# A four-stage kernel of attention, soft experts and a feed-forward network: where the copy of the key rows and the queries' transposing DMA stand, and how the value tails are loaded

## The chip, the cores and the metric

One core of a Trainium2 chip. The metric is the device time of one launch in microseconds (us); three runs of the kernel before took 892.85, 893.1 and 895.21 us, median 893.1.

## The reference

Block-causal attention over 8 batches of 8 heads (576 positions, 64 wide), then a soft mixture of 8 experts with 4 slots each, then a feed-forward network with a squared ReLU:

```python
scores = scale * np.matmul(q, k.transpose(0, 1, 3, 2))
scores = np.where(block_i >= block_j, scores, -1000000000.0)   # blocks of 64 positions
attn = np.exp(scores - np.max(scores, axis=-1, keepdims=True))
attn = attn / (np.sum(attn, axis=-1, keepdims=True) + 1e-09)
x = np.matmul(attn, v)                       # to [4608, 512]
logits = x @ phi                             # 32 slots
d = softmax over the tokens; slot_input = d.T @ x
slot_out[e] = np.maximum(slot_input[e] @ w1[e], 0.0) @ w2[e]
x = softmax over the slots (logits) @ slot_out
h = np.maximum(x @ w_in, 0.0); out = h * h @ w_out
```

## The kernel before, in words

Attention works on pairs of heads: pair n is batch n // 4, and in it heads j and 4 + j with j = n % 4, so there are 32 pairs. A function `pair(n)` (L958) writes one step of a pipeline down: the scores and exponentials of pair n, the row maxima of pair n + 2 (`maxpass`), the preparation of pair n + 3 (`split`), the product with the values of pair n - 1 (`pv`), and the loads of later pairs. It has eight slots; each has some functions to call, then up to four loads from a list `dq` (`loads(LR)`), then bits of other work.

The scores of a pair are two matmuls that add up in PSUM: `s1` against `t1` (the transposed keys, high and low parts, and the transposed high parts of the queries), and `s2` against `t2` (L528). `s1` comes from a transposing DMA of `ka` (L425). `s2` is a copy, by a DMA from SBUF to SBUF, of the first 64 rows of `s1`; its other rows are constants (L925). `t2` comes from a transposing DMA of `qb` (L513), which holds the low parts of the queries, the mask and the row maxima; so it can't start before `maxpass` has ended in `fin`. There are two homes for `s2`, one for each parity of n, and one `t2` for each parity: the DMAs that fill them for pair n wait until the scores of pair n - 2 have been read.

In the kernel before `fin` (slot 5 of pair n - 2) issues the transposing DMA for pair n, and pair n - 1 puts the copy for pair n at the head of the load list in slot 2 (L1040). The values of a pair lie in a home of 640 columns, four such homes taking turns: 4 x 128 rows per head, and the last 64 rows ("tail") of both heads by two DMAs of 64 rows of 64 numbers (L311), one per head, for every pair.

TensorE's instructions stand in the order in which the program writes them (`manual_schedule`, L1059). For the other engines a scheduler chooses the order from what is ready by its own account, with the program's order as the preference; SyncE's queue, from which all these DMAs go out in order, is made by it. Each instruction there waits for its own semaphores, and everything behind it waits too.

The weights of the experts (32 chunks of 1 MB) go through a ring of buffers, many of them memory that attention has given back: `wchunks` (L899) adds their loads when a pool is closed, for instance `st_b` and `st_m` at pair 31. The experts and then the feed-forward network follow when attention is over.

Of the kernel before, what the change touches and what calls it, by code (L numbers as in the profile page):

```python
# [10 lines left out]
F16 = mybir.dt.float16  # L11
# [12 lines left out]
def tile_attn_soft_moe_ffn(  # L24
# [97 lines left out]
        return dict(q=t[:, 0], k=t[:, 1])  # L122

    def v_tile(n):
        c0 = 512 * V0 + 640 * (n % 4)
        return ar_hi[:, c0:c0 + 640].rearrange("p (a h d) -> p a h d", h=2, d=D)

    def wchunk(i):
        kind, g, c = wlist[i]
# [106 lines left out]
    def attention():  # L236
# [63 lines left out]
        def load_v(n):  # L300
            b, j = divmod(n, NJ)
            t = v_tile(n)

            def main(hp):
                nc.sync.dma_start(
                    out=t[:, 0:NU, hp, :], in_=v[b][NJ * hp + j, 0:128 * NU, :].rearrange("(u p) d -> p u d", p=128)
                )

            def tail():
                for h in range(2):  # L310
                    nc.sync.dma_start(out=t[64 * h:64 * h + 64, NU, 0, :], in_=v[b][NJ * h + j, 128 * NU:S, :])  # L311

            return [lambda: main(0), tail, lambda: main(1)]

        def load_phi(hp):
            nc.sync.dma_start(
# [76 lines left out]
        def split(n):  # L393
# [45 lines left out]

            return [high_q, lambda: [turn_q(0, 8), turn_q(8, NBLK)], prep_k, low_q]  # L440

        def maxpass(n):
            t1, s1 = T[n][0], T[n][1]
            pmt = pm[n % 2]
            pf = pmt.rearrange("p a b -> p (a b)")
            ptl = sm_p.tile([128, 5], F32, tag="ptl", name="ptl")
            box = {}

            def part(ps, hp, u, c0):
                nc.tensor.matmul(  # L450
                    ps[:, c0:c0 + 128 * (u + 1)].rearrange("p (s c) -> p s c", c=128), t1[:, 2 * u + hp, :],
                    s1[:, hp:2 * u + 2:2, :], start=(c0 == 0), stop=False,
                )

            def mask(ps, c0, step, cnt):
                o = ps[:, 0:512].rearrange("p (a x) -> p a x", x=128)
                o = o[:, c0 // 128:c0 // 128 + (cnt - 1) * (step // 128) + 1:max(step // 128, 1), 64:128]
                nc.tensor.matmul(o, mrow_l, mrow_r[:, 0:1].to_broadcast([128, 64 * cnt]), start=False, stop=True)  # L458

            def red(ps, o, w, cnt=None):  # L460
                i = ps[:, 0:w].rearrange("p (a x) -> p a x", x=min(128, w))
                if cnt:
                    i = ps[:, 0:w].rearrange("p (c a x) -> p c a x", c=cnt, x=128)
                nc.vector.tensor_reduce(out=o, in_=i, axis=AX.X, op=ALU.max)  # L464

            def chunk(i):
                ps = ps_r.tile([128, 512], F32, tag="r", name="ps_max")
                box[i] = ps
                if i < 2:
                    part(ps, i, 0, 0)  # L470
                    part(ps, i, 2, 128)
                    mask(ps, 0, 384, 2)
                    red(ps, pf[:, 8 * i + 3:8 * i + 7], 512)
                elif i == 2:
                    part(ps, 0, 1, 0)
                    part(ps, 1, 1, 256)
                    mask(ps, 128, 256, 2)
                    red(ps, pmt[:, 4:6, 0:2], 512, 2)
                elif i < 5:
                    part(ps, i - 3, 3, 0)  # L480
                    mask(ps, 384, 128, 1)
                    red(ps, pmt[:, 3 + i, :], 512)
                else:
                    for hp in range(2):
                        h0 = 64 * hp
                        nc.tensor.matmul(
                            ps[h0:h0 + 64, 0:512].rearrange("p (s c) -> p s c", c=128) if i == 5
                            else ps[h0:h0 + 64, 0:64],
                            t1[:, 8, h0:h0 + 64],
                            s1[:, hp:8:2, :] if i == 5 else s1[:, 8, h0:h0 + 64],  # L490
                            start=True, stop=True,
                        )
                    red(ps, ptl[:, 0:4] if i == 5 else ptl[:, 4:5], 512 if i == 5 else 64)

            def fin():
                mx = box[4][:, 0:NBLK]
                mv = mx[:, 0:8].rearrange("p (u h) -> p h u", h=2)
                pv4 = pmt.rearrange("p (a b) c -> p a b c", b=2)
                nc.vector.tensor_reduce(out=mv[:, :, 0:3:2], in_=pv4[:, 0:2], axis=AX.X, op=ALU.max)
                nc.vector.tensor_reduce(  # L500
                    out=mv[:, :, 1:4:2].rearrange("p h u -> p u h"), in_=pv4[:, 2:4], axis=AX.X, op=ALU.max
                )
                nc.vector.tensor_reduce(out=mx[:, 8:9], in_=ptl, axis=AX.X, op=ALU.max)
                t = qb[n % NBQ]
                nc.vector.tensor_scalar(
                    out=t[:, :, 64:65], in0=mx.unsqueeze(2), scalar1=-1.0 / SHIFT, scalar2=None, op0=ALU.mult
                )
                nc.vector.scalar_tensor_tensor(
                    out=t[:, :, 65:66], in0=mx.unsqueeze(2), scalar=-1.0 / SHIFT, in1=t[:, :, 64:65],
                    op0=ALU.mult, op1=ALU.subtract,  # L510
                )
                t2 = (mid, odd)[n % 2].tile([128, NBLK, 128], F16, tag="t2", name="t2")
                nc.sync.dma_start_transpose(out=t2, in_=t.rearrange("p s c -> p (s c)"))  # L513
                T[n][2] = t2

            return [lambda i=i: chunk(i) for i in range(5)] + [fin, lambda: [chunk(5), chunk(6)]]

# [66 lines left out]
        def pv(n):  # L584
# [22 lines left out]
            def tl(t):  # L607
                if t == 0:
                    box["tl"] = ps_v.tile([128, 384], F32, tag="tl", name="tl")
                for hp in range(2):  # L610
                    b_, c_ = pp[hp, 1], pp[hp, 2]
                    r = (b_[:, 0:64], b_[:, 448:512], c_[:, 256:320], c_[:, 448:512], pp["d"][:, hp, :])[t]
                    nc.tensor.matmul(  # L613
                        box["tl"][64 * hp:64 * hp + 64, 320:384], vs[:, t, hp if t < NU else 0, :], r,
                        start=(t == 0), stop=False,
                    )

# [340 lines left out]
        def pair(n):  # L958
# [61 lines left out]
            def at_(i, *fs):  # L1020
                slot.setdefault(i, []).extend(f for f in fs if f)
# [9 lines left out]
            if n == 1:  # L1031
                at_(3, sp[2])
                at_(4, sp[0])
                at_(7, sp[1], sp[3])
            else:
                at_(4, get(sp, 3))
            for i in range(8):
                for f in slot.get(i, []):
                    f()
                if i == 2 and n + 1 < N:  # L1040
                    dq.insert(0, lambda: s2copy(n + 1))
                loads(LR)
                f = aux.pop(0) if aux else None
                if f:
# [605 lines left out]
```

## Time and profile before

| | |
|---|---|
| profiled execution | 892.94 us |
| its span, first to last instruction | 891.2 us |
| mean granted TensorE clock | 0.981 |
| TensorE matmuls busy | 824.0 us (92%) |
| VectorE, ScalarE busy | 668.3 us (75%), 627.6 us (70%) |
| GpSimd busy | 253.9 us (28%) |
| queue q1 (all DMAs of SyncE), packet time | 52.1% of 16 engines' span |

Attention ends at about 440 us of the span, the experts take to about 493, the feed-forward network the rest. The rows below use PE for TensorE, DVE for VectorE, ACT for ScalarE, POOL for GpSimd and SPq for SyncE's queue. L12 is line 12 of the kernel. An engine's busy time is not its value: what counts is which wait ends last.

### The profile page before, as it was taken

Reading aid. Unit: us, or ns where it says so; the run is one execution under the profiler, and the core shown is the slowest. Engines: PE = TensorE matmul, PEld = TensorE weight load, DVE = VectorE, ACT = ScalarE, POOL = GpSimd, SP = SyncE. Lnnn points to the kernel's source line nnn. Section 1 sums busy time; section 2 is a strip of 40 time slices with the busy share of each in tenths; the row PEclk is TensorE's granted clock in tenths of the full one; section 3 lists DMA queues with packets and bytes.
Section 4 is the critical chain, followed back from the end, with each engine's and each line's share of the span. In section 5 each row is a group of like instructions: output and inputs, shape, how many; then the busy total and the mean of one; then the engine's idle time right before and its main releaser. Section 6 shows DMA issues by size and latency. Waiting matters only on the chain.

```text
span 891.2 us, 22012 instructions
## 1 busy us (share of the span) xinstructions
PE 824.0 (92%) x8788; PEld 613.5 (69%) x8788; DVE 668.3 (75%) x1600; ACT 627.6 (70%) x1012; POOL 253.9 (28%) x394
## 2 busy tenths in 40 slices
PE   2778998999999999988997799999999999999997
PEld 1446766656676767665633444788888888888887
DVE  5756777968888888952552999788878888888880
ACT  5478776767878777643313789987788888887870
POOL 0234746648584848563200000000000000000000
PEclk9889999999999999998999899999999999999999
DMA  8887899989889789496999600100010000000002
GB/s 167 158 160 154 165 194 163 198 180 191 165 193 185 174 155 187 95 241 159 327 369 382 274 0 1 48 25 25 26 47 25 25 25 25 25 25 25 25 25 48
DMA packets 222023, 113.18 MB, mean 127 GB/s; under 512 B 193760, under 2 KB 195808, under 8 KB 221920
## 3 DMA queue, kind: packets, MB, share of 16 engines
q1 hardware_dynamic: 219264, 111.12, 52.1%
q8 instruction: 69, 1.13, 0.5%
q10 hardware_dynamic: 2656, 0.66, 0.4%
q14 instruction: 34, 0.28, 0.1%
HBM read 78.71 MB, written 9.44 MB: 99 GB/s over the span
## 4 chain that ended last, share of the span: by engine, by line
PE 65%; DMA 9%; DVE 8%; POOL 7%; ACT 6%; issue 2%; SPq 2%; ACTq 0%
PE ps_y L1464 14%; PE ps_x L1464 9%; PE ps_z L1464 9%; PE xm L602 7%; PE po L1486 4%; PE ps_hb L1428 3%; POOL ss L572 3%; DMA s<-ka 3%; PE ps_sc L529 3%; POOL ul L712 3%; DVE pm L464 3%; PE tl L613 2%; DMA wch<-in_moe_w_dram 2%; PE ps_h L1155 2%; PE ps_max L450 2%
## 5 line engine op out<-in xcount | busy, mean ns | idle before, releaser
L1464 PEld LDWEIGHTS <-ah 128*128 128x128 f16 x1792 | 170.3, 98 | 21.9
L567 ACT ACTIVATE p<-ps_sc,es 128x512 f32<-128x512 f32 x192 | 129.0, 695 | 41.7 <-PE ps_sc L529 25.9
L1397 DVE TENSOR_TENSOR al<-a,ah 128x1024 f16<-128x1024 f32 (+1 forms) x128 | 138.7, 1126 | 16.7 <-ACT ah L1451 15.3
L464 DVE TENSOR_REDUCE pm<-ps_max 128x4 f32<-128x512 f32 x160 | 108.6, 684 | 50.2 <-PE ps_max L458 49.4
L572 POOL TENSOR_TENSOR ss<-p 128x384 f32<-128x384 f32 (+1 forms) x128 | 94.4, 758 | 170.3 <-ACT p L567 169.9
L1451 ACT CAST ah<-a 128x1024 f16<-128x1024 f32 (+1 forms) x128 | 114.4, 936 | 15.0 <-DVE a L1397 13.6
L1557 POOL TENSOR_TENSOR ot<-u,p 128x256 f32<-128x256 f32 x16 | 12.4, 778 | 374.6 <-DVE u L1528 338.9
L529 PE MATMUL ps_sc<-t,s 128*128 128x512 f16 (+3 forms) x512 | 106.4, 302 | 13.0 <-DMA s<-s 6.8
L1464 PE MATMUL ps_y<-bh,ah 128*128 128x256 f16 x384 | 104.9, 273 | 0.0
L1464 PE MATMUL ps_y<-bh,al 128*128 128x256 f16 x384 | 104.7, 273 | 0.0
L1464 PE MATMUL ps_y<-bl,ah 128*128 128x256 f16 x384 | 104.7, 273 | 0.0
L572 POOL TENSOR_TENSOR ss<-ss,p 128x320 f32<-128x320 f32 (+1 forms) x128 | 101.1, 790 | 11.8 <-ACT p L567 3.1
L1319 ACT ACTIVATE r<-ps_hb,alpha 128x1024 f32<-128x1024 f32 x64 | 71.2, 1112 | 34.1 <-PE ps_hb L1428 33.4
L1464 PEld LDWEIGHTS <-al 128*128 128x128 f16 x896 | 87.5, 98 | 10.1
L602 PE MATMUL xm<-p,ar_hi 128*64 128x256 f32 (+3 forms) x512 | 93.8, 466 | 0.0
L1397 DVE TENSOR_TENSOR a<-a 128x256 f32<-128x256 f32 x192 | 76.1, 424 | 3.9
L450 PE MATMUL ps_max<-s,t 128*128 128x128 f16 (+3 forms) x256 | 62.3, 309 | 9.7 <-DMA s<-ka 8.2
L1464 PE MATMUL ps_x<-bh,ah 128*128 128x256 f16 x256 | 70.1, 274 | 0.0
L1464 PE MATMUL ps_z<-bh,ah 128*128 128x256 f16 x256 | 70.0, 273 | 0.0
L1464 PE MATMUL ps_z<-bh,al 128*128 128x256 f16 x256 | 69.8, 273 | 0.0
L1464 PE MATMUL ps_x<-bh,al 128*128 128x256 f16 x256 | 69.8, 273 | 0.0
L1464 PE MATMUL ps_x<-bl,ah 128*128 128x256 f16 x256 | 69.8, 273 | 0.0
(255 smaller groups left out, 1827.7 us busy)
## 6 DMA issues: line engine op xcount, KB each, us to landing
wch<-in_moe_w_dram SPq DMA_DIRECT2D x18, 1024.0 KB, 11.0
ar_hi<-in_v_dram SPq DMA_DIRECT2D x64, 128.0 KB, 3.0
raw<-in_moe_w_in_dram SPq DMA_DIRECT2D x16, 512.0 KB, 4.9
out_dram<-ot SPq DMA_DIRECT2D x32, 256.0 KB, 2.2
ar_hi<-in_moe_w_dram SPq DMA_DIRECT2D x6, 1024.0 KB, 8.9
s<-s SPq DMA_DIRECT2D x32, 144.0 KB, 3.5
ar_lo<-in_k_dram SPq DMA_DIRECT2D x32, 128.0 KB, 3.7
ar_hi<-in_k_dram SPq DMA_DIRECT2D x32, 128.0 KB, 3.3
```

The costliest lines, as they stand in the source:

```text
L450: nc.tensor.matmul(ps[:, c0:c0 + 128 * (u + 1)].rearrange("p (s c) -> p s c", c=128), t1[:, 2 * u + hp, :], s1[:, hp:2 * u + 2:2, :], star ...
L464: nc.vector.tensor_reduce(out=o, in_=i, axis=AX.X, op=ALU.max)
L529: nc.tensor.matmul(ps[:, c0:c0 + w].rearrange("p (s c) -> p s c", c=128), kk[:, 2 * t + hp, :], qq[:, 2 * u0 + hp:8:2, :], start=(c0 == 0 ...
L567: exps[:] = [nc.scalar.activation(out=pt, in_=ps, func=AF.Exp, scale=es[:, 0:1])]
L572: add = lambda o, x, y: nc.gpsimd.tensor_tensor(out=o, in0=x, in1=y, op=ALU.add)
L602: nc.tensor.matmul(box["xm"][64 * hp:64 * hp + 64, 128 * t:512], vs[:, t, hp, :], r, start=(t == 0), stop=(t == 3),)
L712: add = lambda o, x, y: nc.gpsimd.tensor_tensor(out=o, in0=x, in1=y, op=ALU.add)
L1319: nc.scalar.activation(out=r[:, c0:c1], in_=ps[:, c0:c1], func=AF.Relu, **kw)
L1397: sub = lambda o, a, b: nc.vector.tensor_tensor(out=o, in0=a, in1=b, op=ALU.subtract)
L1451: nc.scalar.copy(v(hl[n % 2][0][:, 2 * kq:2 * kq + 2], s), v(a7[n, kq], s))
L1464: nc.tensor.matmul(acc[:, 0:HM], a[:, k], b[:, k], start=bool(first and k + j == 0), stop=(k == KH - 1 and j == 2), skip_group_check=not f ...
L1486: nc.tensor.matmul(pos[t], g[:, 512 * a + 128 * t:512 * a + 128 * t + 128], tt[:, c, a], start=(c == 0 and a == 0), stop=(c == KH - 1 and ...
```

## The change

The copy to `s2` for pair n + 1 is written at the head of pair n, before slot 0, and no longer goes through the load list. The queries' transposing DMA becomes a function of its own, `turn_qb`; for pairs 0 and 1 it is still called by `fin`, for all others at the head of pair n for pair n + 1, right behind the copy. The values' homes shrink to 512 columns, and the tails of a whole batch (four pairs) lie in a home of 256 columns, two of them taking turns; they are loaded by two DMAs of 64 rows of 4 x 64 numbers when the first pair of a batch is loaded. The bytes are the same.

```diff
--- before.py
+++ after.py
@@ -122,8 +122,12 @@
         return dict(q=t[:, 0], k=t[:, 1])
 
     def v_tile(n):
-        c0 = 512 * V0 + 640 * (n % 4)
-        return ar_hi[:, c0:c0 + 640].rearrange("p (a h d) -> p a h d", h=2, d=D)
+        c0 = 512 * (V0 + n % NJ)
+        return ar_hi[:, c0:c0 + 512].rearrange("p (a h d) -> p a h d", h=2, d=D)
+
+    def v_tail(b):
+        c0 = 512 * (V0 + NJ) + 256 * (b % 2)
+        return ar_hi[:, c0:c0 + 256].rearrange("p (j d) -> p j d", d=D)
 
     def wchunk(i):
         kind, g, c = wlist[i]
@@ -306,11 +310,13 @@
                     out=t[:, 0:NU, hp, :], in_=v[b][NJ * hp + j, 0:128 * NU, :].rearrange("(u p) d -> p u d", p=128)
                 )
 
-            def tail():
-                for h in range(2):
-                    nc.sync.dma_start(out=t[64 * h:64 * h + 64, NU, 0, :], in_=v[b][NJ * h + j, 128 * NU:S, :])
-
-            return [lambda: main(0), tail, lambda: main(1)]
+            def tail(hp):
+                nc.sync.dma_start(
+                    out=v_tail(b)[64 * hp:64 * hp + 64],
+                    in_=v[b][NJ * hp:NJ * hp + NJ, 128 * NU:S, :].rearrange("j i d -> i j d"),
+                )
+
+            return [lambda: main(0)] + [lambda hp=hp: tail(hp) for hp in range(2) if j == 0] + [lambda: main(1)]
 
         def load_phi(hp):
             nc.sync.dma_start(
@@ -438,6 +444,11 @@
                 nc.scalar.copy(t1[:, s0:s1_, :].rearrange("p s c -> p (s c)"), ps[:, 0:128 * (s1_ - s0)])
 
             return [high_q, lambda: [turn_q(0, 8), turn_q(8, NBLK)], prep_k, low_q]
+
+        def turn_qb(n):
+            t2 = (mid, odd)[n % 2].tile([128, NBLK, 128], F16, tag="t2", name="t2")
+            nc.sync.dma_start_transpose(out=t2, in_=qb[n % NBQ].rearrange("p s c -> p (s c)"))
+            T[n][2] = t2
 
         def maxpass(n):
             t1, s1 = T[n][0], T[n][1]
@@ -509,9 +520,8 @@
                     out=t[:, :, 65:66], in0=mx.unsqueeze(2), scalar=-1.0 / SHIFT, in1=t[:, :, 64:65],
                     op0=ALU.mult, op1=ALU.subtract,
                 )
-                t2 = (mid, odd)[n % 2].tile([128, NBLK, 128], F16, tag="t2", name="t2")
-                nc.sync.dma_start_transpose(out=t2, in_=t.rearrange("p s c -> p (s c)"))
-                T[n][2] = t2
+                if n < 2:
+                    turn_qb(n)
 
             return [lambda i=i: chunk(i) for i in range(5)] + [fin, lambda: [chunk(5), chunk(6)]]
 
@@ -611,7 +621,7 @@
                     b_, c_ = pp[hp, 1], pp[hp, 2]
                     r = (b_[:, 0:64], b_[:, 448:512], c_[:, 256:320], c_[:, 448:512], pp["d"][:, hp, :])[t]
                     nc.tensor.matmul(
-                        box["tl"][64 * hp:64 * hp + 64, 320:384], vs[:, t, hp if t < NU else 0, :], r,
+                        box["tl"][64 * hp:64 * hp + 64, 320:384], vs[:, t, hp, :] if t < NU else v_tail(b)[:, j, :], r,
                         start=(t == 0), stop=False,
                     )
 
@@ -1034,11 +1044,13 @@
                 at_(7, sp[1], sp[3])
             else:
                 at_(4, get(sp, 3))
+            if n + 1 < N:
+                s2copy(n + 1)
+                if n:
+                    turn_qb(n + 1)
             for i in range(8):
                 for f in slot.get(i, []):
                     f()
-                if i == 2 and n + 1 < N:
-                    dq.insert(0, lambda: s2copy(n + 1))
                 loads(LR)
                 f = aux.pop(0) if aux else None
                 if f:
```

The order of TensorE and GpSimd is the same in both kernels, VectorE's differs in two places and ScalarE's in one, all in the first pairs. SyncE's differs throughout. Names: `s2_0`, `s2_1` are the two homes of the copy, `s1` the transposed keys, `t2` the transposed queries, `wch` and `ar_hi<-in_moe_w1` weights of the experts.

The end of attention on SyncE, from the keys' transposing DMA for pair 31 on; before:

```order
L425 DMA_TRANSPOSE s1_7002<-ka_7000 128x9x128
L311 DMA ar_hi_75<-in_v_dram 64x64 x2
L305 DMA ar_hi_75<-in_v_dram 128x4x64
L167 DMA ar_hi_75<-in_moe_w1_dram 128x4x512 x2
L513 DMA_TRANSPOSE t2_7184<-qb0_138 128x9x128
L167 DMA wch_7201<-in_moe_w1_dram 128x4x512
L167 DMA wch_7202<-in_moe_w1_dram 128x4x512
L925 DMA s2_0_141<-s1_6761 64x1152
L167 DMA ar_hi_75<-in_moe_w1_dram 128x2x512
L167 DMA wch_7438<-in_moe_w1_dram 128x4x512
L513 DMA_TRANSPOSE t2_7408<-qb1_139 128x9x128
L925 DMA s2_1_142<-s1_7002 64x1152
```

and now:

```order
L431 DMA_TRANSPOSE s1_6956<-ka_6954 128x9x128
L309 DMA ar_hi_75<-in_v_dram 128x4x64
L171 DMA ar_hi_75<-in_moe_w1_dram 128x4x512 x2
L935 DMA s2_0_141<-s1_6717 64x1152
L450 DMA_TRANSPOSE t2_7156<-qb0_138 128x9x128
L171 DMA wch_7153<-in_moe_w1_dram 128x4x512
L171 DMA wch_7154<-in_moe_w1_dram 128x4x512
L171 DMA ar_hi_75<-in_moe_w1_dram 128x2x512
L935 DMA s2_1_142<-s1_6956 64x1152
L171 DMA wch_7388<-in_moe_w1_dram 128x4x512
L450 DMA_TRANSPOSE t2_7390<-qb1_139 128x9x128
```

The copy for pair 30 (into `s2_0`) stood behind the transposing DMA for pair 30 and two weight chunks, and now stands ahead of all three; the copy for pair 31 (into `s2_1`), which was the last DMA of attention, stands ahead of one chunk and of the transposing DMA for pair 31.

SyncE around the transposing DMA for pair 9 (`qb0`) and the keys' one for pair 11 that follows it; before:

```order
L305 DMA ar_hi_75<-in_v_dram 128x4x64
L311 DMA ar_hi_75<-in_v_dram 64x64 x2
L305 DMA ar_hi_75<-in_v_dram 128x4x64
L925 DMA s2_1_142<-s1_1744 64x1152
L165 DMA ar_hi_75<-in_moe_w1_dram 128x512
L513 DMA_TRANSPOSE t2_2181<-qb0_138 128x9x128
L327 DMA ar_lo_71<-in_k_dram 128x4x64 x2
L334 DMA ar_lo_71<-in_q_dram 64x4x64 x2
L425 DMA_TRANSPOSE s1_2217<-ka_2215 128x9x128
```

and now:

```order
L309 DMA ar_hi_75<-in_v_dram 128x4x64 x2
L169 DMA ar_hi_75<-in_moe_w1_dram 128x512
L333 DMA ar_lo_71<-in_k_dram 128x4x64 x2
L333 DMA ar_lo_71<-in_q_dram 128x4x64 x2
L935 DMA s2_1_142<-s1_1730 64x1152
L169 DMA ar_hi_75<-in_moe_w1_dram 128x512
L450 DMA_TRANSPOSE t2_2203<-qb0_138 128x9x128
L333 DMA ar_lo_71<-in_k_dram 128x4x64
L340 DMA ar_lo_71<-in_q_dram 64x4x64 x2
L333 DMA ar_lo_71<-in_k_dram 128x4x64
L431 DMA_TRANSPOSE s1_2201<-ka_2199 128x9x128
```

The two DMAs for the value tails are gone from here, and loads of keys, queries and weights that came later stand in this stretch; between the two transposing DMAs at its end there are four loads, as before.

## Rows read from the trace of the kernel before

**Rows 1.** Waits of TensorE, whole span: us in total, times, longest.

```profile
PE ps_max L450 <- DMA s<-ka: 8.2, 5, 2.9
...
PE ps_sc L529 <- DMA s<-s: 6.8, 3, 5.3
...
PE ps_sc L529 <- DMA t<-qb: 4.6, 1, 4.6
```

**Rows 2.** Timeline of TensorE, pair 30: start, us, line, work, idle before.

```profile
398.14 0.38 PE L529 MATMUL ps_sc<-t,s 128*128 128x512 f16 x1
...
403.86 0.61 PE L529 MATMUL ps_sc<-t,s 128*128 128x512 f16 x1 [5.35 <-DMA s<-s]
...
410.56 0.28 PE L639 MATMUL tl<-pd,ones 128*32 128x64 f32 x8
...
418.19 0.61 PE L529 MATMUL ps_sc<-t,s 128*128 128x512 f16 x2
```

**Rows 3.** Timeline of SyncE's queue, end of attention.

```profile
383.34 0.99 SPq L167 DMA_DIRECT2D ar_hi<-in_moe_w_dram  x2
386.99 3.85 SPq L513 DMA_TRANSPOSE t<-qb  x1
390.94 2.10 SPq L167 DMA_DIRECT2D wch<-in_moe_w_dram  x2
393.09 1.70 SPq L925 DMA_DIRECT2D s<-s  x1
...
401.55 2.75 SPq L513 DMA_TRANSPOSE t<-qb  x1
...
416.66 1.49 SPq L167 DMA_DIRECT2D wch<-in_moe_w_dram  x3
```

**Rows 4.** Landings: L513 of 386.99, L925 of 393.09, L513 of 401.55.

```profile
DMA to landing us min/median/max: 9.0/9.0/9.0
...
DMA to landing us min/median/max: 10.7/10.7/10.7
...
DMA to landing us min/median/max: 7.2/7.2/7.2
```

**Rows 5.** Windows: us, busy (instructions) of each engine, clock, DMA share, GB/s.

```profile
403.80:411.00 7.20, 7.14 (x72) 4.07 (x73) 0.00 (x0) 1.35 (x3) 0.00 (x0) 0.56 0.78 161
411.00:418.00 7.00, 6.22 (x76) 4.37 (x74) 3.56 (x12) 4.66 (x11) 5.14 (x8) 1.00 0.04 10
...
463.00:468.00 5.00, 5.00 (x48) 1.50 (x48) 0.22 (x1) 0.00 (x0) 0.00 (x0) 1.00 1.05 384
```

**Rows 6.** The chain that ended last, in the experts.

```profile
465.63 14.58 DMA wch<-in_moe_w_dram
```

**Rows 7.** Timeline of TensorE, pair 29, from value product to sums.

```profile
385.60 1.05 PE L602 MATMUL xm<-p,ar_hi 128*64 128x512 f32 x4
...
389.03 0.29 PE L639 MATMUL tl<-pd,ones 128*32 128x64 f32 x8
```

**Rows 8.** Timeline of GpSimd, partial sums of pair 29.

```profile
400.82 1.52 POOL L572 TENSOR_TENSOR ss<-ss,p 128x320 f32<-128x320 f32 x2
```

**Rows 9.** Waits of TensorE in 70 to 90 and in 125 to 150.

```profile
PE ps_sc L529 <- DMA s<-s: 1.5, 2, 1.1
...
PE ps_max L450 <- DMA s<-ka: 2.4, 1, 2.4
```

**Rows 10.** Timeline of SyncE's queue, pairs 0 and 8.

```profile
29.22 0.51 SPq L925 DMA_DIRECT2D s<-s  x1
...
130.51 1.66 SPq L513 DMA_TRANSPOSE t<-qb  x1
...
134.85 2.33 SPq L425 DMA_TRANSPOSE s<-ka  x1
```

**Rows 11.** The tails' DMAs: issue time in ns, min/median/max.

```profile
L311 SPq DMA_DIRECT2D ar_hi<-in_v_dram x64: 472/587/1401, 12.7 to 382.0; - x64
```

**Rows 12.** Timeline of VectorE, low keys of pair 11.

```profile
129.66 0.80 DVE L418 SCALAR_TENSOR_TENSOR ka<-ar_lo,sig,ka 128x576 f16<-128x576 f32 x1
```

## The prediction

> **What bounds the kernel now.** I read the waits of TensorE first. There the reader is to see that TensorE hardly ever waits for a transfer: all its waits for DMAs in attention are three kinds, the transposed keys (s<-ka), the copy of the key rows (s<-s) and the transposed queries (t<-qb), 19.6 us together [rows 1]. The change touches the last two and, by taking DMA issues off SyncE, may touch the first.
>
> Then the timeline of TensorE around the longest wait. The scores of pair 30 start with a matmul at 398.14, the second one needs the copy s2, and TensorE stands still for 5.35 us until 403.86 [rows 2]. SyncE's timeline says why: two weight chunks of 1 MB each were issued at 390.94, ahead of the copy at 393.09 [rows 3], and the copy took 10.7 us to land [rows 4]. A second price follows: in 403.8 to 411 the granted clock is 0.56 of full, so most of that stretch ran at 1.2 instead of 2.4 GHz, with TensorE busy for 7.14 of its 7.20 us [rows 5]. It had done nothing for 5.3 us before.
>
> Then the windows, to see whether time won there is kept. After 418 the DMA engines are full (share 1.05 in 463 to 468), and the chain ends on a weight transfer of 14.58 us [rows 5, 6]. That stretch is bound by transfers. But in 411 to 418 they are idle (0.04) [rows 5]: the next three weight chunks are issued at 416.66 [rows 3], right after the scores of pair 30 end, because they go into buffers that pair 30 still reads. So the stream's start hangs on TensorE's progress, and what pair 30 gains the stream gains too. The later gates (scores of pair 31, last values) move with it. All behind the stream is unchanged.
>
> **The change part by part.** The sum is made against the profiled execution: 892.94 us, that is 1.74 us around its span of 891.2, and 0.16 under the median of the runs shown (893.1).
>
> *The copy at the pair's head, the end of attention.* The scheduler now puts pair 30's copy before its transposing DMA and before the two 1 MB chunks. It has no new wait of its own: it needs the end of the scores of pair 28, which was over when pair 29's stretch began at 385.60 [rows 7], and the chunks before it in the queue were issued at 383.34 [rows 3]. If it goes out behind them, by about 387, and takes even the 10.7 us of before [rows 4], it lands at 397.7, before 398.5. The queries' transposing DMA, which stood at 386.99 and landed 9.0 us later, at 396.0 [rows 3, 4], gets the copy's issue in front of it, 0.5 us or so, and stays in time. So the 5.35 us go. What is late next: behind the second matmul TensorE does the value product of pair 29 and its sums. The same section a pair earlier, at full clock, went from 385.60 to the last sum at 389.03 + 0.29, 3.72 us [rows 7]. From 398.52 that would end at 402.24. But GpSimd finishes the partial sums of pair 29 only at 400.82 + 1.52 = 402.34 [rows 8], and after that the last group of sums, 0.29 us [rows 7], and the half of the group before it that reads these partial sums are left; I put that half at 0.5. So the section ends at about 403.1. Before it ended at 410.56 + 0.28 = 410.84 [rows 2]. Gain 7.7, of which I count **7.6**. The next wait to look at is pair 31: its transposed queries were issued at 401.55 and landed 7.2 us later, 408.75 [rows 3, 4]. That DMA waits for VectorE and does not move; the scores of pair 31, at 418.2 before [rows 2], now come at about 410.6. Margin 1.8 us, thin but there.
>
> *The same edit earlier on.* In 70 to 90 us two waits for the copy cost 1.5 us [rows 9]; the new queue has those copies ahead of the transposing DMA and not behind the next pair's loads: 1.5 gained, between 0 and 1.5. The first transposing DMA of the queries, on which TensorE waits 4.6 us [rows 1], stood behind a copy's issue of 0.51 us at 29.22 [rows 10], and that copy now stands earlier: 0.5, between 0 and 0.5.
>
> *The transposing DMA at the next pair's head.* In program order it goes three slots later, but its inputs (VectorE's maxima, and the scores that still read its home) are ready at about that time anyway, and in the queue it stands as before, just ahead of the keys' transposing DMA. Its result is wanted a pair later, so 0. The lower bound is a loss: the copy's issue, 0.51 us [rows 10], now sits directly ahead of it and of the keys' one. Were that on the path in each of some 28 pairs, it would be 14 us. I take 0 because TensorE waits for these keys in 5 pairs only [rows 1].
>
> *The tails.* 64 DMAs become 16, and an issue takes 0.587 us in the median [rows 11]. 48 x 0.587 = 28 us of SyncE time, 1.2 us in three pairs of four. It counts only where SyncE is late. Is it? Around 130 us yes: VectorE had the low keys ready at 129.66 + 0.80 = 130.46 [rows 12], their transposing DMA was issued at 134.85 [rows 10], 4.4 us late, and TensorE waited 2.4 us for it [rows 9]. Between them stood the queries' DMA, issued at 130.51 [rows 10], and four loads, and those four stay in the new queue. So what helps is only that SyncE comes to this place earlier. All waits for the keys are 8.2 us [rows 1]; bounds 0 and 8.2, and below 0 if loads that now run ahead of them fill the engines. I take 2.7, a third. The new home has as many bytes, the loads the same rows, the matmuls the same shapes: 0.
>
> A rule speaks against this term. The Trainium skill, page "DMA: Bandwidth & Descriptors", section "Issuing engines are not separate DMA queues", says that the time a sequencer takes to start a DMA is usually small beside the DMA itself. By it the tails would be worth nothing. The case at 130 us disagrees, with 4.4 us of lateness in SyncE's queue alone; whether it does in the other pairs no row tells.
>
> *The sum.* 7.6 is kept whole. The rest is 1.5 + 0.5 + 2.7 = 4.7, and I keep half, 2.4, because GpSimd and VectorE use TensorE's pauses to catch up, as GpSimd did in the one above. 892.94 - 7.6 - 2.4 = **882.9 us**.
>
> **The rivals.**
>
> *Issue time is worth nothing, transfers are the limit.* The keys' and the tails' terms vanish, half of 2.0 stays: 892.94 - 7.6 - 1.0 = 884.3. For it: a share of 1.05 is seen where the engines are full, and attention comes near it in places. Against it: the 4.4 us above. Chance 0.18. The rule named above would have it so.
>
> *All waits for transfers go.* SyncE is nowhere late any more: 7.6 + 1.5 + 0.5 + 8.2 = 17.8, less the catching up of the others, a quarter of 10.2: 892.94 - 15.2 = 877.7. For it: one late queue feeds the next pair's lateness. Against: the loads between stay. Chance 0.14.
>
> *The wait changes its name.* The change moves the copy, but the transposed queries of pair 30 or 31 come last instead. The copy and 2 MB are in front of the first, 1 MB and the copy of pair 31 in front of the second. The margins are 2.5 and 1.8 us. If one of them is late by 5 us, as the copy was, the 7.6 shrink to about 2, the clock falls again, and with 1.0 to 2.4 from elsewhere it ends at 889 to 892. For it: the landing times of 9.0 and 7.2 us; against: both had the same bytes in front before. Chance 0.11.
>
> *The queue's head costs more than its end gives: slower.* The copy stands in front of both transposing DMAs in every pair, with its issue and its bytes, and loads that used to come after are drawn ahead of them. If the keys' transposes, needed first in the next pair, land 0.5 us later and are last in 28 pairs, 14 us are lost against 10 won: 896.9. It decides from 10 / 28 = 0.36 us a pair. For it: five pairs already wait there. Against: the count of issues between the two transposing DMAs does not grow. Chance 0.07.
>
> **How the numbers follow.** The forecast (882.9, own range 880 to 886) has 0.50, the rivals 0.18, 0.14, 0.11 and 0.07. Differences under 0.3%, 2.7 us, can't be told from none in measurements of this kernel. Faster: the forecast, the first two, and half of the third, 0.87; same: most of the other half, 0.05; slower: 0.08. The range is 876 to 889: it holds the forecast and the first two rivals and the edge of the third.
>
> **What would show it.** Right: no wait of over 1 us for s<-s in the whole trace; the window after pair 30's first scores at a clock near 1.0; the three weight chunks that stood at 416.66 issued at 407 to 409; the chain from there as before, 8 to 10 us earlier; the waits for s<-ka under 8.2 us in sum. Wrong: a wait for t<-qb of some us at the start of pair 30 or 31; waits for s<-ka in more than 8 pairs, or over 12 us in sum; the chunks still issued at 414 or later; or the chunks early and the last weight transfer at its old time, which would mean that the transfers, not TensorE, set the start.

## The result

Faster, by more than predicted: median 880.0 us (876.78 to 883.25, four runs) against 893.33 us (892.85 to 895.21, four runs), ratio 0.9847 [0.9801, 0.9893]. 882.9 was predicted, 876 to 889 as the range. The profiled execution took 876.78 us, span 875.0 us. Repeated beside the experiments, the changed kernel gave 878.2 us (874.56 to 884.48, six runs), ratio 0.9846 [0.9813, 0.988].

So the forecast came out, but its sum did not: two of its terms were off in opposite directions, so it is in part luck that it came as near as 3 us. This is what the rest is about.

### The profile page after: what moved, and what is told of

It reads as the page before. It is cut to its first block, busy times and chain, and to the rows that moved or that the text cites. A ratio compares the mean times of both kernels' runs of the same rounds, so it can differ in the third digit from the quotient of the medians.

```text
span 875.0 us, 21966 instructions
## 1 busy us (share of the span) xinstructions
PE 820.3 (94%) x8788; PEld 613.4 (70%) x8788; DVE 668.9 (76%) x1600; ACT 627.6 (72%) x1012; POOL 255.0 (29%) x394
## 4 chain that ended last, share of the span: by engine, by line
PE 68%; POOL 8%; DVE 7%; ACT 7%; DMA 6%; issue 3%; SPq 1%; ACTq 0%; DVEq 0%
PE ps_y L1476 14%; PE ps_x L1476 10%; PE ps_z L1476 10%; PE xm L612 6%; PE po L1498 4%; POOL ss L582 4%; PE ps_sc L539 4%; POOL ul L722 3%; PE ps_hb L1440 3%; DVE pm L475 2%; PE ps_max L461 2%; PE tl L623 2%; PE ps_h L1167 2%; DMA wch<-in_moe_w_dram 2%; DMA ar_hi<-in_moe_w_out_dram 1%
## 5 line engine op out<-in xcount | busy, mean ns | idle before, releaser
L612 PE MATMUL xm<-p,ar_hi 128*64 128x256 f32 (+3 forms) x512 | 87.6, 441 | 0.0
L1476 PE MATMUL ps_z<-bl,ah 128*128 128x256 f16 x256 | 69.8, 273 | 0.0
## 6 DMA issues: line engine op xcount, KB each, us to landing
wch<-in_moe_w_dram SPq DMA_DIRECT2D x18, 1024.0 KB, 10.9
```

What stands on the lines that cost most here:

```text
L612: nc.tensor.matmul(box["xm"][64 * hp:64 * hp + 64, 128 * t:512], vs[:, t, hp, :], r, start=(t == 0), stop=(t == 3),)
L1476: nc.tensor.matmul(acc[:, 0:HM], a[:, k], b[:, k], start=bool(first and k + j == 0), stop=(k == KH - 1 and j == 2), skip_group_check=not f ...
```

## The profile after

Waits of TensorE for DMAs in attention, changed kernel, whole span (us in total, times, longest):

```profile
PE ps_sc L539 <- DMA t<-qb: 4.0, 1, 4.0
PE ps_max L461 <- DMA s<-ka: 2.3, 2, 1.2
```

The wait for the copy (s<-s), 6.8 us before, has no row any more; the one for the keys fell from 8.2 to 2.3 us; the first one for the queries lost 0.6 [rows 1]. SyncE's queue at the end of attention (start, us, line, work):

```profile
372.31 1.03 SPq L171 DMA_DIRECT2D ar_hi<-in_moe_w_dram  x2
374.42 0.47 SPq L935 DMA_DIRECT2D s<-s  x1
376.64 4.17 SPq L450 DMA_TRANSPOSE t<-qb  x1
380.91 2.44 SPq L171 DMA_DIRECT2D wch<-in_moe_w_dram  x2
383.40 1.31 SPq L171 DMA_DIRECT2D ar_hi<-in_moe_w_dram  x1
387.15 0.47 SPq L935 DMA_DIRECT2D s<-s  x1
387.66 0.59 SPq L171 DMA_DIRECT2D wch<-in_moe_w_dram  x1
391.24 2.85 SPq L450 DMA_TRANSPOSE t<-qb  x1
398.57 1.48 SPq L171 DMA_DIRECT2D wch<-in_moe_w_dram  x3
```

Pair 30's copy is issued at 374.42, and still takes this long to land:

```profile
L935 SPq DMA_DIRECT2D s<-s x1: 473/473/473, 374.4 to 374.4; - x1
...
DMA to landing us min/median/max: 10.4/10.4/10.4
```

It landed at 384.8. In the kernel before it was issued at 393.09 and took 10.7 us [rows 3, 4]: the copy became no faster, it only starts 18.7 us earlier. TensorE's timeline of pair 30:

```profile
386.84 0.28 PE L557 MATMUL ps_sc<-t,s 128*128 128x128 f16 x2
386.95 1.04 PE L817 MATMUL ps_x<-ident,xt 128*128 128x128 f32 x8
387.83 0.59 PE L539 MATMUL ps_sc<-t,s 128*128 128x512 f16 x2
...
392.13 0.41 PE L644 MATMUL tl<-ss,ones 128*32 128x128 f32 x8 [0.24 <-POOL ss L582]
...
392.48 0.28 PE L649 MATMUL tl<-pd,ones 128*32 128x64 f32 x2
```

The two first score matmuls now stand together (x2), where one stood alone for 5.35 us before [rows 2]. From there to the last sum it is 392.76 - 387.83 = 4.93 us, against 410.84 - 398.14 = 12.70 before; the prediction had 403.1 - 398.14 = 4.96, with the same wait for GpSimd's partial sums in it. Windows of the changed kernel over this stretch and at the weight stream (us, busy of PE, PEld, DVE, ACT and POOL, clock, DMA share, GB/s):

```profile
386.50:392.00 5.50, 5.39 (x70) 3.46 (x68) 3.06 (x12) 2.22 (x4) 5.01 (x12) 1.00 1.05 385
392.00:398.00 6.00, 5.87 (x80) 4.44 (x80) 2.88 (x11) 4.32 (x10) 3.47 (x6) 1.00 1.17 254
...
438.00:443.00 5.00, 5.00 (x52) 1.60 (x48) 0.50 (x2) 0.60 (x1) 0.00 (x0) 1.00 1.04 386
```

The clock stays at 1.00 where it was 0.56, and behind the last sums the transfers run at a share of 1.17 (392 to 398), where behind the last sums of before they stood at 0.04 for 7 us [rows 5]. The chain's last transfers:

```profile
447.80 14.11 DMA wch<-in_moe_w_dram
464.21 13.07 DMA ar_hi<-in_moe_w_out_dram
```

The weight transfer that was at 465.63 [rows 6] is 17.8 us earlier.

**Where along the program the time is won.** The table is worked out from TensorE's timelines: the start of the last score matmul of a pair in the kernel before (profiled execution), and how much earlier, in us, that same matmul starts in the other profiled executions (the experiments are below).

| pair | before, us | after | full_again | before_again | v_tails_only | e_end_only | full_minus_end | split4_issues | ct_no_tails | c_copy_only |
|---|---|---|---|---|---|---|---|---|---|---|
| 2 | 68.74 | 1.2 | 1.3 | 0.8 | 1.1 | -0.8 | 1.1 | -4.1 | -0.3 | -1.5 |
| 8 | 136.08 | 3.1 | 3.2 | -0.6 | 2.7 | 0.2 | 2.9 | -8.6 | -0.5 | 0.1 |
| 9 | 152.22 | 6.0 | 6.1 | 1.0 | 4.8 | 2.5 | 5.9 | -5.0 | -0.8 | 1.2 |
| 11 | 176.78 | 6.0 | 6.1 | 1.0 | 4.8 | 2.5 | 5.9 | -7.3 | -0.7 | 1.2 |
| 12 | 191.80 | 9.9 | 10.0 | 1.1 | 8.6 | 5.7 | 9.8 | -4.8 | 3.1 | 5.1 |
| 29 | 397.14 | 10.3 | 10.6 | 1.2 | 8.5 | 5.2 | 8.0 | -11.2 | 3.1 | 3.8 |
| 30 | 416.34 | 18.1 | 18.4 | 3.0 | 10.7 | 13.1 | 11.4 | -9.3 | 10.9 | 11.6 |
| end | 892.94 | 16.2 | 18.4 | 1.8 | 11.5 | 9.4 | 11.7 | -11.4 | 10.5 | 8.7 |

Two things stand in it. The end of attention gives what was worked out: 18.08 - 10.30 = 7.78 us between pairs 29 and 30. But 10.3 us are won before it, where the prediction had 2.4. And the kernel before is not one fixed thing: its own second trace is 1.2 us earlier at pair 29, and e_end_only, whose queue is that of before until pair 29, is 5.2 us earlier there. Its gains at pairs 9 and 12, 2.3 and 3.2 us, stand beside 3.0 and 3.9 of the changed kernel. So the size of a step in this table depends on the one trace of before that it is measured from. The two traces of the changed kernel agree within 0.3 us from pair 2 to pair 30.

**What one of these steps is made of.** Between pairs 8 and 9 the gain grows by 2.96 us, between 11 and 12 by 3.87. Those two stretches in the kernel before (columns as above):

```profile
136.08:152.22 16.14, 13.63 (x169) 9.54 (x167) 11.08 (x28) 10.39 (x23) 9.00 (x15) 0.89 0.95 155
...
176.78:191.80 15.02, 12.95 (x166) 7.61 (x164) 8.31 (x26) 8.82 (x17) 4.92 (x7) 0.89 0.84 180
```

and the same two in the changed kernel:

```profile
133.01:146.19 13.18, 11.95 (x169) 8.88 (x167) 11.18 (x28) 10.40 (x23) 9.34 (x15) 1.00 0.89 182
...
170.75:181.90 11.15, 11.15 (x167) 7.23 (x165) 8.24 (x26) 8.84 (x17) 4.93 (x7) 1.00 0.97 185
```

The same matmuls were busy 12.95 us and are now busy 11.15: 1.80 us of the 3.87 is the clock, 0.89 against 1.00 in the mean of the stretch. The other 2.07 is TensorE's idle time, which is one wait in the kernel before:

```profile
139.46 0.39 PE L450 MATMUL ps_max<-s,t 128*128 128x128 f16 x2 [2.38 <-DMA s<-ka]
...
181.29 0.55 PE L450 MATMUL ps_max<-s,t 128*128 128x128 f16 x2 [2.07 <-DMA s<-ka]
```

Between 8 and 9 it is 1.28 us of idle time (2.38 became 1.10) and 1.68 of slower matmuls. So a pause of 2 us cost nearly twice its length. It does not always: in before_again the stretch from pair 8 to 9 had a wait of 2.5 us for the keys, in v_tails_only one of 2.0, and the clock stayed at 1.00 in both.

How the keys came earlier here can be read from SyncE's queue at the second of these waits, before:

```profile
164.47 1.12 SPq L311 DMA_DIRECT2D ar_hi<-in_v_dram  x2
...
170.06 3.99 SPq L513 DMA_TRANSPOSE t<-qb  x1
174.16 0.52 SPq L909 DMA_DIRECT2D raw<-in_moe_w_in_dram  x1
174.77 2.00 SPq L425 DMA_TRANSPOSE s<-ka  x1
```

and after:

```profile
164.41 2.80 SPq L450 DMA_TRANSPOSE t<-qb  x1
167.30 0.54 SPq L309 DMA_DIRECT2D ar_hi<-in_v_dram  x1
167.94 2.14 SPq L431 DMA_TRANSPOSE s<-ka  x1
```

VectorE had the low keys ready at 172.71 before and at 166.69 after. Their transposing DMA was issued 2.06 us after that, and is now issued 1.25 us after it: 0.8 us won in the queue. And it landed 6.48 us after its issue (181.25), and now 4.3: 2.2 won in the transfer. At the wait of 139.46 the two shares are about equal, 0.66 and 0.63. But these are two DMAs in one execution of each kernel: in e_end_only, with the queue of before, the one of the second wait landed in 5.1 us.

All 32 of the keys' transposing DMAs tell the shares apart. Lateness is the time from the end of VectorE's low keys to the issue, mean of the 32, worked out from the timelines; the landing is the median. SyncE's share is the sum of its DMAs' issue times up to the end of the last copy's issue, over that time.

| run | tails' DMAs | SyncE's share | lateness, us | landing, us | TensorE's waits for s<-ka, us |
|---|---|---|---|---|---|
| before | 64 | 0.82 | 1.8 | 4.2 | 8.2 |
| before_again | 64 | 0.81 | 1.6 | 4.1 | 7.5 |
| e_end_only | 64 | 0.83 | 1.9 | 4.1 | 5.4 |
| ct_no_tails | 64 | 0.83 | 1.9 | 4.2 | 9.4 |
| c_copy_only | 64 | 0.83 | 1.8 | 4.3 | 4.1 |
| after | 16 | 0.76 | 1.2 | 4.1 | 2.3 |
| full_again | 16 | 0.75 | 1.0 | 4.3 | 3.3 |
| v_tails_only | 16 | 0.75 | 1.1 | 4.5 | 3.7 |
| full_minus_end | 16 | 0.75 | 1.2 | 4.1 | 4.7 |
| split4_issues | 128 | 0.84 | 1.5 | 3.9 | 4.8 |

With 16 tails' DMAs the keys go out 0.4 to 0.9 us less late than with 64, in every trace; the landing is no shorter. So the lighter queue paid in the issue, and the shorter landing at the two waits above belongs to these executions. TensorE's waits follow on average (3.5 against 6.9 us), but vary so much that the two groups overlap.

## The experiments

All ratios are against the kernel before in runs on the same chip: 890.97 us (16 runs) for the first four, 892.05 (11) for the next four, 892.35 (23) for the last two. These three sets ran from 886.92 to 897.03 in all, wider than the 2.7 us that the prediction took as what can't be told from none.

**The end alone.** The kernel before, with the copy at the pair's head for pairs 30 and 31 only.

```diff
+            if N - 2 <= n + 1 < N:
+                s2copy(n + 1)
             for i in range(8):
...
-                if i == 2 and n + 1 < N:
+                if i == 2 and n + 1 < N - 2:
                     dq.insert(0, lambda: s2copy(n + 1))
```

> The kernel before, with the copy at the head of the pair for pairs 30 and 31 alone; SyncE's queue is otherwise that of before up to pair 29. Theory (the copy of pair 30 waits behind two 1 MB chunks, and the weight stream starts when pair 30 ends): the 5.35 us wait goes, the clock stays full in the 7 us behind it, the three chunks of 416.66 are issued 7.5 to 8 us earlier, and the time falls by 7 to 8 us, to 885.5. Rival (the transfers set the end of the experts, so that what attention wins there is given back): the wait goes, the last weight transfer lands at most 4 us earlier, and the time is 889 or more.

Measured: 886.04 us (882.32 to 890.49, ten runs), ratio 0.9951 [0.9926, 0.9977], 4.4 us where 7 to 8 were expected. In the trace the step at pair 30 is whole, 7.9 us (table: 13.1 - 5.2), but 3.7 us of the gain at pair 30 are gone at the end of the program. The mechanism is there, its price in time is smaller than in the trace of before.

**The tails alone.** The kernel before with the new home and the two DMAs per batch; copy and transposing DMA as before.

```diff
-            def tail():
-                for h in range(2):
-                    nc.sync.dma_start(out=t[64 * h:64 * h + 64, NU, 0, :], in_=v[b][NJ * h + j, 128 * NU:S, :])
+            def tail(hp):
+                nc.sync.dma_start(
+                    out=v_tail(b)[64 * hp:64 * hp + 64],
+                    in_=v[b][NJ * hp:NJ * hp + NJ, 128 * NU:S, :].rearrange("j i d -> i j d"),
+                )
```

> The value tails by two DMAs per batch in their own home, the copy and the transposing DMA where they were. Theory (SyncE's queue is late, 0.59 us per issue): the two waits for the keys at pairs 9 and 12 (2.4 and 2.1 us) shrink to under half, pairs 9 and 12 gain together 4 to 7 us with the clock that comes back, the 5.35 us wait for the copy of pair 30 stays as it is, and the time falls by 5 to 7 us, to 887. Rival (issue time is worth nothing, transfers are the limit): the waits stay and the time is 892 to 894.

Measured: 885.0 us (879.18 to 887.06, five runs), ratio 0.9926 [0.9892, 0.996], 6.6 us [3.6, 9.6]. Its waits:

```profile
PE ps_sc L535 <- DMA s<-s: 4.9, 2, 4.6
PE ps_sc L535 <- DMA t<-qb: 4.0, 1, 4.0
...
PE ps_max L456 <- DMA s<-ka: 3.7, 3, 2.0
```

The copy's wait at pair 30 is still there (4.6), and the time fell as expected. Of the two waits of the expectation the one at pair 12 is gone, but the one at pair 9 is still 2.0: what this trace gains there over that of before is mostly a clock that did not fall. The gain builds up at the same pairs as in the full change, but so does that of e_end_only (table), so the timed runs and the lateness carry this reading, and not the steps. By medians this edit is worth more than the end of attention (6.6 against 4.4 us); the two intervals overlap.

**Copy and transposing DMA, tails as before; and the copy alone.** The second of these leaves out the `turn_qb` lines.

```diff
+            if n + 1 < N:
+                s2copy(n + 1)
+                if n:
+                    turn_qb(n + 1)
             for i in range(8):
...
-                if i == 2 and n + 1 < N:
-                    dq.insert(0, lambda: s2copy(n + 1))
```

> The copy and the queries' transposing DMA at the head of the pair, the tails by two DMAs per pair as before. Theory (the tails' issues made the queue late): the end gains 7.7, the early waits for the copy 1.5, the waits for the keys stay at 4 us or more in sum, and the time is 882 to 885. Rival (the new place of the copy and the order that comes with it removed the keys' waits too): the waits for the keys sum to 2.5 us or less, and the time is that of the whole change, 876 to 881.

> The copy at the head of the pair alone; the transposing DMA is issued behind the row maxima as before, the tails too. Theory (moving the transposing DMA is worth nothing): within 2 us of the kernel with both moved. Rival (the transposing DMA in its old place goes out ahead of the copy and holds it up): slower than that kernel by 3 us or more, with a wait for s<-s of over 1 us somewhere.

Measured: 883.63 us (879.69 to 885.08, four runs), ratio 0.9917 [0.9884, 0.995], and 885.5 us (881.64 to 887.62, six runs), ratio 0.9932 [0.9896, 0.9968]. The two can't be told apart, so the transposing DMA's move is worth nothing that is measured here. Both have the 7.8 us step at pair 30. With both at the head and the tails as before, the keys' waits are no shorter than before:

```profile
PE ps_max L455 <- DMA s<-ka: 9.4, 7, 3.8
```

With the copy alone they are 4.1 us, at the same lateness; single sums of waits don't decide here.

**The full change again, and before again.**

> The whole change once more, for a second trace and a better interval. Theory (the end's 7.8 us are the change's own, the 3.0 and 3.9 us at pairs 9 and 12 are partly chance of one execution, since a kernel with the old order up to pair 29 had gained 5.2 us there too): the step at pair 30 is 7.6 to 8 us again, what is gained up to pair 29 differs by 1 us or more from the 10.3 us of the first trace, and the time is 10 to 14 us under that of before. Rival (all of it is the change's own): up to pair 29 again 10 to 10.6 us.

> The kernel before once more, for a second trace. Theory (chance of one execution in the middle of attention): the wait for the copy of pair 30 is there again with 4.5 to 5.5 us, the waits for the keys differ from 8.2 us by 2 us or more, and pair 29 ends 2 us or more away from 397. Rival (executions agree): pair 29 within 0.5 us of 397, the waits for the keys 8 to 8.5 us.

Measured: 878.2 us (ratio above), and 891.1 us in one run. The expectation of full_again did not come, its rival did: the steps of the changed kernel at pairs 9 and 12 came back within 0.1 us. The changed kernel repeats itself, then; how large the steps are still hangs on the trace of before (above). before_again lies between its two expectations: 1.2 us away at pair 29, the keys' waits 7.5 us. Its wait for the copy was 4.9 us.

**The full change without its end.** The copies of pairs 30 and 31 go back to the load list.

```diff
             if n + 1 < N:
-                s2copy(n + 1)
+                if n + 1 < N - 2:
+                    s2copy(n + 1)
                 if n:
...
+                if i == 2 and N - 2 <= n + 1 < N:
+                    dq.insert(0, lambda: s2copy(n + 1))
```

> The whole change, but the copies for pairs 30 and 31 back in the load list in slot 2 (behind the two weight chunks in SyncE's queue). Theory (the end is worth 7.6 in attention, of which the weight stream keeps what it kept in the kernel with the end alone, 4.4 of 7.8): 4 to 8 us slower than the whole change, with a wait for the copy of 4 to 5.5 us at pair 30. Rival (all that the end wins is given back in the transfers): within 2 us of the whole change.

Measured: 881.86 us (879.98 to 885.26, six runs), ratio 0.9888 [0.986, 0.9916]: 3.7 us slower than the full change by medians, on the same chip, which with six runs of each is uncertain by some 3.5 us. The expectation was 4 to 8. The wait came back, smaller than expected:

```profile
PE ps_sc L539 <- DMA s<-s: 3.2, 1, 3.2
```

Everything ahead of the end is worth 10.0 us [7.5, 12.5], and the end the rest.

**More issues, same bytes.** The kernel before with each pair's tails by four DMAs of 32 rows: 64 more issues.

```diff
-                for h in range(2):
-                    nc.sync.dma_start(out=t[64 * h:64 * h + 64, NU, 0, :], in_=v[b][NJ * h + j, 128 * NU:S, :])
+                for h in range(4):
+                    nc.sync.dma_start(out=t[32 * h:32 * h + 32, NU, 0, :], in_=v[b][NJ * (h // 2) + j, 128 * NU + 32 * (h % 2):128 * NU + 32 * (h % 2) + 32, :])
```

> The kernel before with each pair's value tails loaded by four DMAs of 32 rows and not by two of 64: the same bytes and rows, 64 issues more on SyncE. Theory (SyncE's queue is late where TensorE waits for keys): waits for the keys over 10 us in sum, and 3 to 9 us slower than before. Rival (issue time is small beside the transfers and hidden): the waits for the keys within 2 us of before, and the time within 2 us.

Measured: 907.92 us (904.31 to 913.43, four runs), ratio 1.0181 [1.0142, 1.022], 16.1 us slower. Issue times of the tails' DMAs (ns, min/median/max) here:

```profile
L311 SPq DMA_DIRECT2D ar_hi<-in_v_dram x128: 333/420/1897, 12.4 to 393.9; - x128
```

and in the changed kernel:

```profile
L314 SPq DMA_DIRECT2D ar_hi<-in_v_dram x16: 600/607/1487, 12.3 to 324.2; - x16
```

Summed over the trace these are 63.8 us of SyncE's time, against 37.5 before and 10.7 after. 26 us more of it cost 16 us; 26 us less gave 6.6 in v_tails_only. The time is beyond the 3 to 9 us expected, and it did not come by the keys: their waits are 4.8 us in sum and not over 10, their DMAs no later than before. It went to the copies, which wait behind these issues:

```profile
PE ps_sc L529 <- DMA s<-s: 17.4, 8, 4.8
...
PE ps_max L450 <- DMA s<-ka: 4.8, 3, 3.3
```

Both experiments on the tails change how many DMAs there are, at the same bytes. What an issue costs SyncE and what else a DMA may cost are not separated by them.

**Issues moved to ScalarE's queue.** If SyncE's issue time were all, taking more from it should give more. In the full change the 64 main loads of the values, or the 70 loads of the queries from pair 4 on (56 main ones and 14 tails), are issued by ScalarE:

```diff
             def main(hp):
-                nc.sync.dma_start(
+                nc.scalar.dma_start(
...
+            if n > 3:
+                by = dict(q=nc.scalar)
             for nm in "kq":
```

(The first two lines are one kernel, the last three the other.)

> The whole change, with the values' main loads (64 DMAs) issued by ScalarE and not by SyncE. Theory (what is left of the waits for the keys, 3.3 us, comes from SyncE's queue, and ScalarE has room for 64 issues of 0.5 us): the waits for the keys under 1.5 us, 2 to 5 us faster than the whole change. Rival (ScalarE's exponentials are held up by the issues, or by a wait for a free home in front of them): ScalarE's time is on the path, 2 us or more slower than the whole change.

> The whole change, with the queries' loads (64 main ones and the tails) issued by ScalarE from pair 4 on; these loads are seven pairs ahead and wait for nothing. Theory: as with the values on ScalarE, the waits for the keys under 1.5 us, 2 to 5 us faster than the whole change. Rival (an issue on ScalarE costs as much as it saves on SyncE): within 2 us of the whole change or slower.

Measured: 896.83 us (891.36 to 903.43, twelve runs), ratio 1.006 [1.0031, 1.0089], and 895.5 us (890.81 to 898.81, ten runs), ratio 1.0026 [0.9998, 1.0054]. Both lose the whole gain of the change, and both expectations of a gain failed. An issue is short there (ns, min/median/max, values' loads):

```profile
L309 ACTq DMA_DIRECT2D ar_hi<-in_v_dram x64: 374/375/454, 5.9 to 386.2; - x64
```

But the first wait for the queries grows, and the trace falls back in the first pairs already, 6.7 and 9.9 us against full_again at pair 0. Values' loads on ScalarE, then queries' loads on ScalarE:

```profile
PE ps_sc L539 <- DMA t<-qb: 7.9, 1, 7.9
```

```profile
PE ps_sc L541 <- DMA t<-qb: 10.9, 1, 10.9
```

By pair 29 they are 15.7 and 22.7 us behind, the rest in steps over attention.

The beginning can be followed with the values on ScalarE. Their loads start to go out at 5.93 and not, as in full_again, at 11.41; the keys' first transposing DMA is issued at 16.22 and lands 5.7 us later, at 21.9, where it was issued at 13.78 and landed at 17.3; and the queries' first one goes out at 35.41 and not at 29.66. Loads that leave the one queue are no longer held back to their place in it. That these loads slowed the keys' is argued from this order, not shown, since ScalarE, which prepares the keys too, was also later (its first high keys at 13.56 and not at 12.12).

There is a second candidate, the rival of the first expectation: by the traces ScalarE itself stood still for DMAs, 7.0 us in three waits with the values' loads (ending between 94 and 317 us) and 10.4 us in one with the queries' (ending at 38.8), where full_again has no such wait after the start. SyncE did gain: the keys' DMAs were 0.7 and 0.8 us late in the mean, and 1.0 in full_again. So SyncE's issue time isn't the price by itself. Whether the order of the transfers or ScalarE's waits took the gain is not shown.

## Why the prediction was right, and where its sum was wrong

- *The end of attention, 7.6 kept whole.* The mechanism was right in each step: the copy goes out ahead of the 2 MB, lands in time, the wait of 5.35 us is gone, the clock stays at 1.00, GpSimd's partial sums come last (0.24 us), and pair 31's transposed queries are in time (issued at 391.24, landed 7.4 us later at 398.6, needed at 400.11). The step is 7.78 us in the trace, and 7.8 to 7.9 in all seven traces with the copy at the head, each measured from the first trace of before. Its size in timed runs is smaller: 4.4 us alone [2.1 to 6.6], 3.7 on top of the rest. Part of that is the reference. The wait was 5.35 us in the trace that the sum was made from, and 4.9, 4.8, 4.6 and 3.2 in the four others where the copy stands late; measured from these the step is 6.0 (before_again), 5.9, 5.6 and 4.4 us. The clock behind the wait differs too: in the 7.2 us after it 0.56 was granted in the first trace of before, and 0.76 to 0.78 in the four others. So the sum took the longest wait and the deepest fall of the clock for the usual ones. The other part is lost in the weight stream after attention, where the profiled gains change by -3.7 to +0.8 us; that stays open, as it is seen with and without the edit.
- *The three weight chunks of 416.66 at 407 to 409:* they came at 398.57, 18.1 us earlier. They do hang on TensorE's progress, as was said; TensorE was 10.3 us further along than the end alone explains.
- *The rest, 4.7 halved to 2.4: the step that failed.* It is the term of the keys' waits, 2.7 as "a third" of 8.2, and then "I keep half", because GpSimd and VectorE would use the pauses to catch up. Measured: 10.0 us [7.5, 12.5] for everything ahead of the end, of which the tails alone are 6.6. Two things were wrong in it. The waits went from 8.2 and 7.5 us in two traces of the kernel before to 2.3 and 3.3 in two of the changed one, by more than half and not by a third. And the pauses were not refunded by the others' catching up: what is won by pair 12 (9.9 us) is still there at pair 29 (10.3), and at pairs 9 and 12 of the trace of before, at pair 12 alone of before_again, a pause cost 1.7 to 1.8 us on top in slower matmuls. The prediction counted just this surcharge at the end of attention, and forgot it for the small pauses. How much of the 6.6 us is waits and how much is clock is not shown.
- *The sum.* 10.0 was predicted and 13.7 us (ratio 0.9847) measured. The end was sized 3 to 4 us too high, the rest 7 to 8 too low. The change splits into two kernels that were timed: copy and transposing DMA without the tails 0.9917, the tails alone 0.9926; the product is 0.9844, and the full change had 0.9847 and 0.9846. The first part is 7.4 us, where the prediction had 7.6 + 1.0; the second 6.6 [3.6, 9.6], where it had half of 2.7. So the tails are the term that was far off.
- *Moving the transposing DMA, 0:* nothing that can be measured (0.9932 against 0.9917). *The copy's earlier waits, 2.0 before halving:* no wait for s<-s is left; they weren't timed apart. The first wait for the queries is 0.6 shorter, as taken, but not for the reason given: it is 4.0 us in v_tails_only too, where the copy stands in its old place, and 4.8 and 5.0 in ct_no_tails and c_copy_only, where it stands early. It went with the tails.
- *The rival that issue time is worth nothing* is wrong by two experiments, as far as they tell an issue from what else a DMA costs: 48 issues less gave 6.6 us, 64 more of the same bytes cost 16. The rule behind it (the Trainium skill, page "DMA: Bandwidth & Descriptors", section "Issuing engines are not separate DMA queues") says two things. That issue time is usually small beside the DMA holds for one tail, 0.587 us against a landing of 2.9 us; here SyncE issues for 0.82 of attention, and 48 fewer brought the keys' DMAs out earlier. That several issuers save only sequencer time is not contradicted, but the saving needn't reach the kernel's time: v_on_act took 64 issues off SyncE and came out 0.6% above the kernel before.
- *All waits for transfers go* was the rival nearest to this: 2.3 of the 8.2 us stayed, and 3.3 in the second trace. *The wait changes its name* and *slower* didn't come: no late t<-qb, keys' waits in two pairs and not in 28.

## What to carry to other kernels

Where one queue issues everything in order, look at each small DMA that the busiest engine waits for, and ask what stands ahead of it: bulk transfers, and also many small issues, since both delayed it here. Price a pause of TensorE from the stretch behind it, idle time and slower matmuls together, and don't discount it because other engines use the pause. Make the sum against more than one trace of the kernel before where the wait in question varies from one execution to the next, and compare all of a kind of DMA before reading a cause from one of them.

## What was unexpected of the hardware

- The same DMA from SBUF to SBUF took 2.3 us to land at best, 3.5 in the median and 10.4 with weight chunks around it; at the end of attention, put ahead of two 1 MB chunks but then behind two others, it took 10.4 in place of 10.7 us.
- The issue of a transposing DMA held SyncE for 1.25 to 4.17 us in the same kernel, with the same shape.
- A pause of about 2 us brought the mean clock of a pair's stretch to 0.89 in one execution and left it at 1.00 in another.
- SyncE was issuing DMAs for 0.82 of attention; 48 small ones less brought the keys' transposing DMAs out 0.4 to 0.9 us earlier in the mean, and changed their landing by nothing that can be seen.
